# Transposing batch 1's first attention half by DMA, with later value loads and an earlier second pass, in a Sinkhorn-attention and gated-FFN kernel

## The chip, the cores and the metric

The kernel runs on one core of a Trainium2 chip. The metric is the device time of one execution in microseconds, the median of several runs; lower is better. Durations below come from one profiled execution.

## The reference

The first half is block-sorted attention over 4 batches, 8 heads, 768 positions, head size 64. The second half is a gated FFN on its output, read as 3072 tokens of 512.

```python
for _ in range(5):                      # P = sort_net, 8 x 8 for each batch and head
    P = exp(P - max(P)); P = P / rowsum(P); P = P / colsum(P)
k_sorted, v_sorted = P applied to the 8 blocks (of 96 positions) of k and v
attn = softmax(q_block @ k_sorted_block.T / 8)      # 96 x 96, block by block
x = (attn @ v_sorted_block), heads side by side     # 3072 x 512
out = (silu(x @ w_gate) * (x @ w_val)) @ w_out      # 512 -> 1536 -> 512
```

## The kernel before

**The FFN is cut into eight passes** of 384 tokens, pass n = 2b + half for batch b. In a pass, `gate` (L382) and `value` (L400) each make one of twelve 128-row groups of the hidden layer: four matmuls that read x of the pass, transposed, from the tile `xts[(b, half)]`, one matmul for each quarter (kc = 0 to 3) of the 512 features. `outp` (L414) multiplies by w_out, for the tokens of the pass before (`outp(n - 1, ...)`), so the last output comes after the last pass, in `out_halves` (L430).

**Attention is spread between the FFN's matmuls.** A unit is a pair of heads and one half of the sequence, four units make the x of one pass, eight make a batch. A unit goes through `scores` (L294, tile qk), `exps` (L314, ScalarE), `av` (L325: matmuls into av_ps, then reciprocal and product on VectorE into the tile st, L339 and L341), and then a transposition of st into one quarter of `xts`. There are two ways to transpose: `xtr` (L355) does it with four TensorE transposes (L352) and a VectorE copy; `x_dma` (L363) with one transposing DMA from SyncE's queue (L367). Batch 0 and batch 1's first half (units 0 to 3) use `xtr`; batch 1's second half and batches 2 and 3 use `x_dma`. Feature quarter kc of `xts` comes from unit kc of the half.

**Keys, queries and values.** `kq_chunk` (L239, tile tkq) mixes keys and rearranges queries of batch 1 in three pairs of chunks, each pair 64 matmuls, with one PSUM tile emptied by VectorE and one by ScalarE. `v_chunk` (L269, tile tv) mixes batch 1's values in four chunks of 16 matmuls, which read `vch`, a copy of the values with the positions innermost; GpSimd writes vch (`copy_v`, L117, run at L124). For batches 2 and 3 keys and values are loaded as pairs, `v_pair_chunk` mixes the values, and the queries go another way: `q_cast` (L370) casts them DRAM to DRAM into q_scr with GpSimd's DMA queue, in runs of 64 elements, and `q_dma` (L374) transposes q_scr into kqtq from SyncE's queue.

**Order.** TensorE's and GpSimd's instructions run in the order in which they are written. `merge` (L570) writes it: the main list is the FFN's pass, each entry with a cost (0.65 for a gate or value group, 0.87 for a third of an output tile), and a side entry is placed behind the main entry with which the summed cost reaches its due time. `units`, `kqs` and `vs` give the side entries; L609 sets the due times of pass 1, the subject here. PSUM tiles with tag "a" or "b" have one buffer each, so a matmul into one waits until the last content has been read. The order on VectorE, ScalarE and SyncE from pass 0 on is the scheduler's. GpSimd's queue, in order: copies of batch 1's values into vch (L596), the loads of the key pair (L598), of values 2 and 3 (L599), the two query casts (L601), and the four copies of the value pair into vch (L611).

Of the kernel before, what the change touches and what calls it, by code (L numbers as in the profile page):

```python
# [9 lines left out]
FP32 = mybir.dt.float32  # L10
BF16 = mybir.dt.bfloat16
# [6 lines left out]
def kernel(  # L18
# [11 lines left out]
    nc = tc.nc  # L30

    B, H, S, D = q.shape
    NB = sort_net.shape[-1]
    C = S // NB
    BH = B * H
    H2 = H // 2
    scale = 1.0 / float(D) ** 0.5
    N_ITER = 5
    DM = moe_w_gate.shape[0]
# [4 lines left out]
    R = H * NB  # L44

    k_nat = k.rearrange("b h (j c) d -> b (h j) c d", c=C)
    q_nat = q.rearrange("b h (j c) d -> b (h j) c d", c=C)
    v_nat = v.rearrange("b h (j c) d -> b (h j) c d", c=C)
# [5 lines left out]
    const = ctx.enter_context(tc.tile_pool(name="const", bufs=1))  # L54
    natp = ctx.enter_context(tc.tile_pool(name="natp", bufs=2))
    vnp = ctx.enter_context(tc.tile_pool(name="vnp", bufs=1))
    kqp = ctx.enter_context(tc.tile_pool(name="kqp", bufs=2))
    vtp = ctx.enter_context(tc.tile_pool(name="vtp", bufs=2))
    ssp = ctx.enter_context(tc.tile_pool(name="ssp", bufs=3))
    xtp = ctx.enter_context(tc.tile_pool(name="xtp", bufs=4))  # L60
    wpool = ctx.enter_context(tc.tile_pool(name="wpool", bufs=1))
    hpool = ctx.enter_context(tc.tile_pool(name="hpool", bufs=2))
# [1 line left out]
    opool = ctx.enter_context(tc.tile_pool(name="opool", bufs=3))  # L64
# [18 lines left out]
    kq_tiles = {}  # L83
    v_tiles = {}

    def kq_tile(b):
        if b not in kq_tiles:
            kq_tiles[b] = natp.tile([128, C, D], BF16, name=f"kq{b}", tag="nat")
        return kq_tiles[b]

    def load_k(b, lo, hi):
        rows = highr if b else lowr
        nc.gpsimd.dma_start(out=kq_tile(b)[rows, lo:hi, :], in_=k_nat[b, :, lo:hi, :])

    def load_k_pair():
        kq_tiles["p"] = natp.tile([128, C, D], BF16, name="kp", tag="nat")
        for u in range(2):
            nc.gpsimd.dma_start(out=kq_tiles["p"][u * R:(u + 1) * R], in_=k_nat[2 + u])

    def load_q(b, lo, hi):  # L100
        rows = lowr if b else highr
        nc.gpsimd.dma_start(out=kq_tile(b)[rows, lo:hi, :], in_=q_nat[b, :, lo:hi, :])

    def load_v(b, lo, hi):
        if b // 2 not in v_tiles:
            v_tiles[b // 2] = vnp.tile([128, C, D], BF16, name=f"v{b // 2}", tag="vn")
        u = b % 2
        nc.gpsimd.dma_start(out=v_tiles[b // 2][u * R:(u + 1) * R, lo:hi], in_=v_nat[b, :, lo:hi, :])

    def load_w(sb, dram, lo, hi):  # L110
        nc.gpsimd.dma_start(out=sb[:, :, lo:hi], in_=dram[:, :, lo:hi])
# [1 line left out]
    def load_gv(lo, hi):  # L113
        load_w(wg_sb, wg_dram, lo, hi)
        load_w(wv_sb, wv_dram, lo, hi)

    def copy_v(eng, pair, rows, s, n=4, d0=0, d1=D):  # L117
        cs = slice(s * (C // n), (s + 1) * (C // n))
        dst = vch3[rows, d0:d1, cs]
        src = v_tiles[pair][rows, cs, d0:d1]  # L120
        if eng is nc.scalar:
            eng.copy(dst, src.transpose([0, 2, 1]))  # L122
        else:
            eng.tensor_copy(dst, src.transpose([0, 2, 1]))  # L124

    ident = const.tile([128, 128], BF16)
    lowr, highr = slice(0, R), slice(R, 2 * R)
# [5 lines left out]
    HC = C // 2  # L133
    QC = C // 4
    halves = (lowr, highr)
    qk0 = natp.tile([128, C, D], BF16, name="qk0", tag="nat")
    k0 = qk0[:, 0:HC, :]
    q0 = [qk0[:, HC + t * QC:HC + (t + 1) * QC, :] for t in range(2)]
    q_runs = q.rearrange("b h (t r c) d -> b t r h (c d)", t=2, c=QC)
# [1 line left out]
    def load_q0(t):  # L141
        nc.gpsimd.dma_start(out=q0[t].rearrange("p c d -> p (c d)"), in_=q_runs[0, t])

    load_v(0, 0, HC)
    load_v(0, HC, C)
    make_identity(nc, ident)
    load_q0(0)
    for a, rows in enumerate(halves):
# [5 lines left out]
    load_q0(1)  # L154
    load_gv(512, 1024)
    load_gv(1024, DF)
    load_v(1, 0, HC)
    load_v(1, HC, C)
    for lo, hi in ((0, 64), (64, C)):
        load_k(1, lo, hi)  # L160
        load_q(1, lo, hi)
    for n in range(3):
# [28 lines left out]
    def bank_tile(name, tag="gen"):  # L191
        return psum.tile([128, 512], FP32, name=name, tag=tag, bufs=3 if tag == "gen" else 1)
# [20 lines left out]
    for lo in (0, NB // 2):  # L213
        part = slice(lo, lo + NB // 2)
# [6 lines left out]
    def drain(eng, dst, src):  # L221
        if eng == "v":
            nc.vector.tensor_copy(dst, src)  # L223
        else:
            nc.scalar.copy(dst, src)  # L225
# [3 lines left out]
    def kqt_tile(b):  # L229
        if b not in kqts:  # L230
            kqts[b] = kqp.tile([128, 2 * H2 * NB * C + 32], BF16, name=f"kqt{b}", tag="kqt")
        return kqts[b]
# [3 lines left out]
    def chunk_tile(name, n, tag):  # L236
        return pair_tile(name, tag) if n == 2 else bank_tile(name, tag)

    def kq_chunk(b, at, n, eng, tag):  # L239
        dst = kqt_tile(b)[:, 0:2 * GI * C].rearrange("p (n c) -> p n c", c=C)  # L240
        rm = rmix[b].rearrange("p a (g two) i -> p two (a g) i", two=2)
        tp = chunk_tile("tkq", n // 8, tag).rearrange("p (l n) -> p l n", n=2 * GI)
        for lc in range(n):
            for two in range(2):
                nc.tensor.matmul(tp[two * D:(two + 1) * D, lc, :],  # L245
                                 lhsT=kq_tiles[b][:, at + lc, :],
                                 rhs=rm[:, two], start=True, stop=True)
        drain(eng, dst[:, :, at:at + n], tp.transpose([0, 2, 1]))

# [41 lines left out]
    es, sts, xts = {}, {}, {}  # L291
# [32 lines left out]
    def qk(b, u, tag="b"):  # L324
        exps(b, u, *scores(b, u, tag))  # L325
# [104 lines left out]
    def out_halves(n, t3):  # L430
        b, half = divmod(n, 2)
        base = b * S + half * TW + t3 * 128
        for part, eng in ((0, "s"), (1, "v")):
            cols = slice(part * DM // 2, (part + 1) * DM // 2)
            o_ps = bank_tile("o_ps")[:, 0:DM // 2]
            for m in range(NFC):
                nc.tensor.matmul(o_ps, lhsT=h_tiles[n][:, m, ts(t3, 128)], rhs=wo_sb[m // 4][:, m % 4, cols],  # L437
                                 start=(m == 0), stop=(m == NFC - 1))
            o_sb = opool.tile([128, DM // 2], FP32, name="oh_sb", tag="oh_sb")
            drain(eng, o_sb, o_ps)  # L440
            nc.sync.dma_start(out=out[ds(base, 128), cols], in_=o_sb)

    idle_ps = bank_tile("idle_ps", "x")

# [46 lines left out]
    for b in range(1, B):  # L491
        rows = halves[b % 2]
# [46 lines left out]
    man = tc.manual_schedule(engines={ET.PE, ET.Pool})  # L539
    man.__enter__()  # L540

    def units(b, us, ats, lags=(3.1, 3.1)):
        us = list(us)
        todo = []
        for n, at in enumerate(ats):
            u, u2 = us[2 * n:2 * n + 2]
            lag = lags[n]
            held = []
            todo.append((at, lambda u=u, u2=u2, held=held: (qk(b, u, "b"), held.append(scores(b, u2, "a")))))
            todo.append((at + 1.3, lambda u2=u2, held=held: exps(b, u2, *held[0])))  # L550
            for w, tag, t in ((u, "b", 1.9), (u2, "a", 3.6)):
                if b == 0 or b == 1 and u < H2:
                    todo.append((at + t, lambda w=w, tag=tag: av(b, w, tag)))
                    todo.append((at + t + lag, lambda w=w: drain("v", *xtr(b, w))))
                else:
                    todo.append((at + t, lambda w=w, tag=tag: (av(b, w, tag), x_dma(b, w))))
        return todo

    def kqs(b, ats):
        return [(at, lambda n=n: (kq_chunk(b, n * 32, 16, "v", "b"), kq_chunk(b, n * 32 + 16, 16, "s", "a")))  # L560
                for n, at in enumerate(ats)]

    def vs(f, size, ats):
        return [(at, lambda m=m: f(1, m * size, size, "sv"[m % 2], "ba"[m % 2])) for m, at in enumerate(ats)]

    def v_pairs(ats):
        return [(at, lambda m=m: (v_pair_chunk(1, m * 16, 8, "v", "b"), v_pair_chunk(1, m * 16 + 8, 8, "s", "a")))
# [2 lines left out]
    def merge(main, side):  # L570
        done, k = 0.0, 0
        side = sorted(side, key=lambda t: t[0])
        for c, f in main:
            f()
            done += c
            while k < len(side) and side[k][0] <= done:
                side[k][1]()
                k += 1
        while k < len(side):
            side[k][1]()  # L580
            k += 1

    def ffn(n):
        todo = []
        for m in range(NFC):
            if n > 0 or m > 1:
                todo.append((0.65, lambda m=m: gate(n, m)))
            if n > 0 or m > 0:
                todo.append((0.65, lambda m=m: value(n, m)))
            ends = (7, 9, 11) if n == 1 else (3, 7, 11)  # L590
            if n > 0 and m in ends:
                for part in range(3):
                    todo.append((0.87, lambda t3=ends.index(m), part=part: outp(n - 1, t3, part)))
        return todo

    for s in range(4):  # L596
        copy_v(nc.gpsimd, 0, highr, s)
    load_k_pair()  # L598
    load_v(2, 0, C)  # L599
    load_v(3, 0, C)  # L600
    q_cast(2)  # L601
    q_cast(3)
    both = slice(0, 128)
    def q0_rest():
        q0_chunk(1, 0, 16, "s", "b")
        q0_chunk(1, 16, 8, "v", "a")

    merge(ffn(0), [(0.0, q0_rest)] + units(0, range(4, 8), (2.0, 6.6)))
    merge(ffn(1), kqs(1, (4.6, 5.9, 10.4)) + vs(v_chunk, 16, (7.2, 7.9, 8.5, 9.1))  # L609
          + units(1, range(4), (11.7, 16.4), (3.1, 2.4)))  # L610
    for s in range(4):  # L611
        copy_v(nc.gpsimd, 1, both, s)
    nc.vector.memset(kqt_tile("p")[:, 2 * GI * C:], 0.0)
# [42 lines left out]
```

## Time and profile before

| what | value |
|---|---|
| median of 3 runs (lowest to highest) | 248.76 us (248.68 to 249.51) |
| profiled execution, its own time | 248.79 us |
| its span in the trace | 246.7 us |
| TensorE, share of the span busy | 96% |
| pass 1 (first gate matmul to first gate matmul of pass 2) | 43.11 to 76.99 us |
| pass 2, likewise | 76.99 to 107.05 us |
| last matmul's group ends, last copy | 243.66, 243.68 to 244.1 us |
| software DMA queue (GpSimd's), moved | 14.16 MB |

The profile page gives busy time by engine, the span in 40 slices, the DMA queues, the chain of work that ended last, and groups of instructions by source line. The trace answers closer questions: instructions in order of time, waits and who ended them, stretches of time with DMA rates, and for each DMA the time from issue to landing. A row of the instruction listing reads: start, duration, engine, line, operation, tiles and shapes, count, and in brackets the idle time before it and what ended that.

### The profile page before, as it was taken

Reading aid. Unit: us, or ns where it says so; the run is one execution under the profiler, and the core shown is the slowest. Engines: PE = TensorE matmul, PEld = TensorE weight load, DVE = VectorE, ACT = ScalarE, POOL = GpSimd, SP = SyncE. Lnnn points to the kernel's source line nnn. Section 1 sums busy time; section 2 is a strip of 40 time slices with the busy share of each in tenths; the row PEclk is TensorE's granted clock in tenths of the full one; section 3 lists DMA queues with packets and bytes.
Section 4 is the critical chain, followed back from the end, with each engine's and each line's share of the span. In section 5 each row is a group of like instructions: output and inputs, shape, how many; then the busy total and the mean of one; then the engine's idle time right before and its main releaser. Section 6 shows DMA issues by size and latency. Waiting matters only on the chain.

```text
span 246.7 us, 6160 instructions
## 1 busy us (share of the span) xinstructions
PE 236.6 (96%) x2609; PEld 140.3 (57%) x2633; DVE 157.7 (64%) x332; ACT 109.8 (45%) x186; POOL 50.3 (20%) x44
## 2 busy tenths in 40 slices
PE   6799999998999999999999999999999999999995
PEld 6375666575555566655555655565555555555543
DVE  6786779888455685867557746755764585446700
ACT  3977653364444444354642642254245334222311
POOL 5992139990098000000000000000000000000000
PEclk9999999999999999999999999999999999999999
DMA  5989999999999195110121111112111211100122
GB/s 96 215 121 208 206 220 210 203 224 222 183 183 161 40 201 127 45 45 0 45 74 35 58 58 35 44 43 78 32 43 45 50 48 53 43 27 20 43 82 88
DMA packets 36682, 24.38 MB, mean 99 GB/s; under 512 B 27696, under 2 KB 32560, under 8 KB 36272
## 3 DMA queue, kind: packets, MB, share of 16 engines
q0 software_dynamic: 18480, 14.16, 37.6%
q1 hardware_dynamic: 18176, 9.84, 14.2%
q8 instruction: 20, 0.33, 0.5%
q14 instruction: 6, 0.05, 0.1%
HBM read 28.32 MB, written 7.86 MB: 147 GB/s over the span
## 4 chain that ended last, share of the span: by engine, by line
PE 84%; DVE 7%; issue 3%; ACT 2%; DMA 2%; DVEq 0%; POOLq 0%
PE g_ps L386 24%; PE v_ps L404 24%; PE o_ps L421 23%; PE tkq L245 3%; PE qk L308 3%; PE av_ps L335 3%; DMA v<-in_v_dram 2%; DVE st L341 2%; DVE vt L223 1%; DVE gs_sb L396 1%; PE o_ps L437 1%; DVE h L409 1%; PE idle_ps L447 1%; PE tv L276 1%; PE x_ps L352 1%
## 5 line engine op out<-in xcount | busy, mean ns | idle before, releaser
L396 DVE SCALAR_TENSOR_TENSOR gs_sb<-th_sb,g_ps 128x384 bf16<-128x384 bf16 x96 | 52.9, 551 | 46.6 <-ACT th_sb L394 43.5
L404 PE MATMUL v_ps<-xt,wv_sb 128*128 128x384 bf16 x380 | 77.3, 326 | 0.1
L386 PE MATMUL g_ps<-xt,wg_sb 128*128 128x384 bf16 x376 | 76.6, 325 | 0.2
L394 ACT ACTIVATE th_sb<-g_ps 128x384 bf16<-128x384 f32 x96 | 47.2, 491 | 57.7 <-PE g_ps L386 55.1
L421 PE MATMUL o_ps<-wo,h 128*128 128x512 bf16 x255 | 62.1, 379 | 1.3 <-issue 0.3
L409 DVE SCALAR_TENSOR_TENSOR h<-v_ps,gs_sb 128x384 bf16<-128x384 f32 x96 | 53.3, 556 | 7.1
L404 PEld LDWEIGHTS <-wv_sb 128*128 128x128 bf16 x380 | 35.4, 97 | 23.9 <-issue 1.0
L386 PEld LDWEIGHTS <-wg_sb 128*128 128x128 bf16 x376 | 35.0, 97 | 24.3 <-issue 0.6
L421 PEld LDWEIGHTS <-h 128*128 128x128 bf16 x276 | 25.8, 98 | 27.9
L426 ACT COPY o_sb<-o_ps 128x512 f32<-128x512 f32 x23 | 13.5, 586 | 45.2 <-PE o_ps L421 45.2
L124 POOL COPY vch<-v 64x1536 bf16<-64x1536 bf16 (+2 forms) x11 | 28.7, 2639 | 14.1 <-DMA v<-in_v_dram 14.0
L321 ACT ACTIVATE e_all<-qk 96x768 bf16<-96x768 f32 x30 | 22.5, 802 | 8.4 <-PE qk L308 8.4
L341 DVE TENSOR_TENSOR st<-av_ps,r_sb 96x512 bf16<-96x512 f32 x32 | 21.7, 680 | 0.2
L335 PEld LDWEIGHTS <-e_all 96*128 96x128 bf16 x256 | 11.9, 98 | 4.9 <-ACT e_all L321 0.9
L339 DVE RECIPROCAL r_sb<-av_ps 96x8 f32<-96x8 f32 x32 | 6.4, 199 | 12.3 <-PE av_ps L335 12.2
L335 PE MATMUL av_ps<-vt,e_all 96*128 96x65 bf16 x256 | 13.1, 193 | 0.1
L223 DVE CAST vt<-tv 96x1024 bf16<-96x1024 f32 (+1 forms) x9 | 9.8, 1098 | 2.6 <-PE tv L286 1.7
L225 ACT CAST vt<-tv 96x1024 bf16<-96x1024 f32 (+1 forms) x9 | 8.1, 914 | 5.5 <-PE tv L286 3.6
L447 PE MATMUL idle_ps<-warm_sb 128*128 128x512 bf16 x22 | 6.1, 381 | 0.4 <-issue 0.2
L223 DVE COPY oh_sb<-o_ps 128x256 f32<-128x256 f32 x1 | 0.4, 425 | 9.3 <-PE o_ps L437 9.3
L371 POOL DMA_DIRECT2D q_scr<-in_q_dram x2 | 5.7, 3232 | 0.0
L122 ACT COPY vch<-v 64x768 bf16<-64x768 bf16 (+1 forms) x4 | 5.5, 1387 | 0.3 <-DMA v<-in_v_dram 0.3
(80 smaller groups left out, 133.1 us busy)
## 6 DMA issues: line engine op xcount, KB each, us to landing
out_dram<-o_sb SPq DMA_DIRECT2D x23, 256.0 KB, 2.0
v<-in_v_dram POOLq DMA_DIRECT2D x4, 384.0 KB, 12.7
wg_sb<-in_moe_w_gate_dram POOLq DMA_DIRECT2D x3, 512.0 KB, 11.3
wv_sb<-in_moe_w_val_dram POOLq DMA_DIRECT2D x3, 512.0 KB, 13.1
wo<-in_moe_w_out_dram POOLq DMA_DIRECT2D x3, 512.0 KB, 15.8
kp<-in_k_dram POOLq DMA_DIRECT2D x2, 768.0 KB, 10.0
v<-in_v_dram POOLq DMA_DIRECT2D x2, 768.0 KB, 16.5
q_scr<-in_q_dram POOLq DMA_DIRECT2D x2, 768.0 KB, 25.0
```

Source lines behind the costliest of these rows:

```text
L124: eng.tensor_copy(dst, src.transpose([0, 2, 1]))
L223: nc.vector.tensor_copy(dst, src)
L321: nc.scalar.activation(e_all[:, n:n + 2, 0:4 * C], wide[0:C, :, 0:4 * C], AF.Exp, scale=scale)
L335: nc.tensor.matmul(o[:, two, i4, 0:D + 1], lhsT=e[:, i4 * C:i4 * C + 128], rhs=vt[:, 2 * g + two, half * 4 + i4, 0:D + 1], start=True, sto ...
L341: nc.vector.tensor_tensor(st.rearrange("p i two d -> p two i d"), o[0:C, :, :, 0:D], r_sb.to_broadcast([C, 2, 4, D]), op=ALU.mult)
L386: nc.tensor.matmul(g_ps, lhsT=wg_sb[:, kc, ts(m, 128)], rhs=xt[:, kc, :], start=(kc == 0), stop=(kc == NKC - 1))
L394: nc.scalar.activation(th_sb, g_ps, AF.Tanh, scale=0.5)
L396: nc.vector.scalar_tensor_tensor(gs_sb, th_sb, 1.0, g_ps, op0=ALU.add, op1=ALU.mult)
L404: nc.tensor.matmul(v_ps, lhsT=wv_sb[:, kc, ts(m, 128)], rhs=xt[:, kc, :], start=(kc == 0), stop=(kc == NKC - 1))
L409: nc.vector.scalar_tensor_tensor(h_tiles[n][:, m, :], v_ps, 0.5, gs_tiles.pop(m), op0=ALU.mult, op1=ALU.mult)
L421: nc.tensor.matmul(o_ps, lhsT=h_w[:, m, ts(t3, 128)], rhs=wo_sb[part][:, m % 4, :], start=(m == 0), stop=(m == NFC - 1))
L426: nc.scalar.copy(o_sb, o_ps)
```

## The change

Seven edits:

1. Batch 1's units 0 to 3 use `x_dma` instead of `xtr`; only batch 0 still transposes on TensorE.
2. Pass 1's due times: the three `kq_chunk` pairs move from 4.6, 5.9, 10.4 to 0.6, 3.3, 7.8; the value chunks from 7.2, 7.9, 8.5, 9.1 to 5.2, 6.5, 9.1, 10.4, with three of four emptied by ScalarE instead of two; the units from 11.7 and 16.4 to 11.0 and 15.6, with the two `av` 1.3 and 2.6 behind the scores instead of 1.9 and 3.6.
3. The loads of values 2 and 3 move behind a one-element GpSimd copy (`hold`) that reads unit 3's quarter of `xts[(1, 0)]`, so they are issued when that transposing DMA has landed. The query casts move up behind the key pair's loads.
4. Tiles for k, q and v are cut into four groups of 24 positions with 16 elements of padding between groups, so that a load's row of a partition is up to four pieces; batch 0's tiles stay dense.
5. The pool of st and r_sb has 4 buffers instead of 3.
6. In `out_halves`, the second half of the last tile is emptied as two quarters, one by VectorE with SyncE's queue, one by ScalarE with ScalarE's own DMA queue.
7. The loads' `lo, hi` are given in groups: k and q of batch 1 come as 48 + 48 positions instead of 64 + 32.

```diff
-    ssp = ctx.enter_context(tc.tile_pool(name="ssp", bufs=3))
+    ssp = ctx.enter_context(tc.tile_pool(name="ssp", bufs=4))
...
+    GC = C // 4
+    def nat_tile(pool, name, tag):
+        return pool.tile([128, 4, GC * D + 16], BF16, name=name, tag=tag)
...
+    def load_groups(tile4, rows, src, lo, hi):
+        nc.gpsimd.dma_start(out=tile4[rows, lo:hi, 0:GC * D],
+                            in_=src[:, lo * GC:hi * GC, :].rearrange("p (s c) d -> p s (c d)", c=GC))
...
-            o_sb = opool.tile([128, DM // 2], FP32, name="oh_sb", tag="oh_sb")
-            drain(eng, o_sb, o_ps)
-            nc.sync.dma_start(out=out[ds(base, 128), cols], in_=o_sb)
+            if part == 0:
+                o_sb = opool.tile([128, DM // 2], FP32, name="oh_sb", tag="oh_sb")
+                drain(eng, o_sb, o_ps)
+                nc.sync.dma_start(out=out[ds(base, 128), cols], in_=o_sb)
+                continue
+            for e, queue, lo in (("v", nc.sync, 0), ("s", nc.scalar, DM // 4)):
+                o_sb = opool.tile([128, DM // 4], FP32, name=f"oq_{e}", tag=f"oq_{e}", bufs=1)
+                drain(e, o_sb, o_ps[:, lo:lo + DM // 4])
+                queue.dma_start(out=out[ds(base, 128), ds(DM // 2 + lo, DM // 4)], in_=o_sb)
...
-    def units(b, us, ats, lags=(3.1, 3.1)):
+    def units(b, us, ats, avs=(1.9, 3.6), lag=3.1):
...
-                if b == 0 or b == 1 and u < H2:
+                if b == 0:
...
-        return [(at, lambda m=m: f(1, m * size, size, "sv"[m % 2], "ba"[m % 2])) for m, at in enumerate(ats)]
+        return [(at, lambda m=m: f(1, m * size, size, "sssv"[m], "ba"[m % 2])) for m, at in enumerate(ats)]
...
     load_k_pair()
-    load_v(2, 0, C)
-    load_v(3, 0, C)
     q_cast(2)
     q_cast(3)
...
-    merge(ffn(1), kqs(1, (4.6, 5.9, 10.4)) + vs(v_chunk, 16, (7.2, 7.9, 8.5, 9.1))
-          + units(1, range(4), (11.7, 16.4), (3.1, 2.4)))
+    merge(ffn(1), kqs(1, (0.6, 3.3, 7.8)) + vs(v_chunk, 16, (5.2, 6.5, 9.1, 10.4))
+          + units(1, range(4), (11.0, 15.6), (1.3, 2.6)))
+    hold = const.tile([1, 1], BF16)
+    nc.gpsimd.tensor_copy(hold, xts[(1, 0)][0:1, H2 - 1, 0:1])
+    load_v(2, 0, 4)
+    load_v(3, 0, 4)
     for s in range(4):
         copy_v(nc.gpsimd, 1, both, s)
```

More of the change, by code (lines that the diff above doesn't have):

```diff
@@ L84, with grouped, dense, kq_at @@
     v_tiles = {}
+    GC = C // 4
+    def nat_tile(pool, name, tag):
+        return pool.tile([128, 4, GC * D + 16], BF16, name=name, tag=tag)
+    def grouped(t):
+        return t[:, :, 0:GC * D].rearrange("p s (c d) -> p s c d", d=D)
+    def dense(t):
+        return t.rearrange("p s n -> p (s n)")[:, 0:C * D].rearrange("p (c d) -> p c d", d=D)
+    def load_groups(tile4, rows, src, lo, hi):
+        nc.gpsimd.dma_start(out=tile4[rows, lo:hi, 0:GC * D],
+                            in_=src[:, lo * GC:hi * GC, :].rearrange("p (s c) d -> p s (c d)", c=GC))
     def kq_tile(b):
         if b not in kq_tiles:
-            kq_tiles[b] = natp.tile([128, C, D], BF16, name=f"kq{b}", tag="nat")
+            kq_tiles[b] = nat_tile(natp, f"kq{b}", "nat")
         return kq_tiles[b]
+    def kq_at(b, c):
+        return grouped(kq_tiles[b])[:, c // GC, c % GC, :]
     def load_k(b, lo, hi):
-        rows = highr if b else lowr
-        nc.gpsimd.dma_start(out=kq_tile(b)[rows, lo:hi, :], in_=k_nat[b, :, lo:hi, :])
+        load_groups(kq_tile(b), highr, k_nat[b], lo, hi)
     def load_k_pair():
-        kq_tiles["p"] = natp.tile([128, C, D], BF16, name="kp", tag="nat")
         for u in range(2):
-            nc.gpsimd.dma_start(out=kq_tiles["p"][u * R:(u + 1) * R], in_=k_nat[2 + u])
+            load_groups(kq_tile("p"), slice(u * R, (u + 1) * R), k_nat[2 + u], 0, 4)
     def load_q(b, lo, hi):
-        rows = lowr if b else highr
-        nc.gpsimd.dma_start(out=kq_tile(b)[rows, lo:hi, :], in_=q_nat[b, :, lo:hi, :])
-    def load_v(b, lo, hi):
[L105 to L108, printed above, removed]
+        load_groups(kq_tile(b), lowr, q_nat[b], lo, hi)
+    def v_tile(pair):
+        if pair not in v_tiles:
+            v_tiles[pair] = nat_tile(vnp, f"v{pair}", "vn")
+        return v_tiles[pair]
+    def load_v(b, lo, hi):
+        rows = slice(b % 2 * R, (b % 2 + 1) * R)
+        if b == 0:
+            nc.gpsimd.dma_start(out=dense(v_tile(0))[rows, lo * GC:hi * GC], in_=v_nat[0, :, lo * GC:hi * GC, :])
+        else:
+            load_groups(v_tile(b // 2), rows, v_nat[b], lo, hi)
     def load_w(sb, dram, lo, hi):
@@ L119, in copy_v @@
         dst = vch3[rows, d0:d1, cs]
-        src = v_tiles[pair][rows, cs, d0:d1]
+        src = (dense(v_tiles[0])[rows, cs, d0:d1] if rows == lowr else
+               grouped(v_tiles[pair])[rows, s, :, d0:d1])
         if eng is nc.scalar:
@@ L135 @@
     halves = (lowr, highr)
-    qk0 = natp.tile([128, C, D], BF16, name="qk0", tag="nat")
+    qk0 = dense(nat_tile(natp, "qk0", "nat"))
     k0 = qk0[:, 0:HC, :]
@@ L142, in load_q0 @@
         nc.gpsimd.dma_start(out=q0[t].rearrange("p c d -> p (c d)"), in_=q_runs[0, t])
-    load_v(0, 0, HC)
-    load_v(0, HC, C)
+    load_v(0, 0, 2)
+    load_v(0, 2, 4)
     make_identity(nc, ident)
@@ L156 @@
     load_gv(1024, DF)
-    load_v(1, 0, HC)
-    load_v(1, HC, C)
-    for lo, hi in ((0, 64), (64, C)):
+    load_v(1, 0, 2)
+    load_v(1, 2, 4)
+    for lo, hi in ((0, 2), (2, 4)):
         load_k(1, lo, hi)
@@ L245, in kq_chunk @@
                 nc.tensor.matmul(tp[two * D:(two + 1) * D, lc, :],
-                                 lhsT=kq_tiles[b][:, at + lc, :],
+                                 lhsT=kq_at(b, at + lc),
                                  rhs=rm[:, two], start=True, stop=True)
@@ L546, in units @@
             u, u2 = us[2 * n:2 * n + 2]
-            lag = lags[n]
             held = []
@@ L550, in units @@
             todo.append((at + 1.3, lambda u2=u2, held=held: exps(b, u2, *held[0])))
-            for w, tag, t in ((u, "b", 1.9), (u2, "a", 3.6)):
-                if b == 0 or b == 1 and u < H2:
+            for w, tag, t in ((u, "b", avs[0]), (u2, "a", avs[1])):
+                if b == 0:
                     todo.append((at + t, lambda w=w, tag=tag: av(b, w, tag)))
```

## Prediction, made before the changed kernel was run

> **What bounds the kernel now.** First the page: busy time by engine, clock and DMA slices, then the chain's shares.
>
> ```profile
> PE 236.6 (96%) x2609; PEld 140.3 (57%) x2633; DVE 157.7 (64%) x332; ACT 109.8 (45%) x186; POOL 50.3 (20%) x44
> ...
> PEclk9999999999999999999999999999999999999999
> DMA  5989999999999195110121111112111211100122
> ...
> PE 84%; DVE 7%; issue 3%; ACT 2%; DMA 2%; DVEq 0%; POOLq 0%
> ```
>
> TensorE is busy 96% of the span, at full clock, and is 84% of the chain; its order is fixed. A microsecond less in its stream is a microsecond less at the end. The DMA engines are full for 13 of 40 slices, to about 80 us, so whatever is added to them before that queues.
>
> Second, TensorE's instructions in order of time through pass 1 (43.11 to 76.99 us, 33.88). Starts tell more than durations, as matmuls overlap: start to start, a gate or value group takes 0.65, a third of an output tile 0.87, a key chunk pair 1.13, a value chunk 0.46, a pair of scores 0.45, an av 0.25, a unit's four transposes 0.17. Pass 1 has 24, 9, 3, 4, 2, 4 and 4 of them: 15.6 + 7.8 + 3.4 + 1.85 + 0.9 + 1.0 + 0.7 = 31.25. So 2.6 us of the 33.88 are gaps. The largest are in these rows:
>
> ```profile
> 56.02 0.63 PE L276 MATMUL tv<-rmix,vch 128*128 128x64 bf16 x16
> 56.84 0.63 PE L276 MATMUL tv<-rmix,vch 128*128 128x64 bf16 x16 [0.20 <-DVE vt L223]
> ...
> 58.70 0.95 PE L245 MATMUL tkq<-rmix,kq 128*64 128x64 bf16 x48
> 60.17 0.44 PE L245 MATMUL tkq<-rmix,kq 128*64 128x64 bf16 x16 [0.52 <-issue]
> ...
> 67.80 0.34 PE L308 MATMUL qk<-kqt 64*128 64x96 bf16 x8
> 68.49 0.34 PE L308 MATMUL qk<-kqt 64*128 64x96 bf16 x8 [0.35 <-DVE st L341]
> ...
> 71.57 0.33 PE L352 MATMUL x_ps<-ident,st 96*128 96x96 bf16 x4
> 71.74 0.81 PE L404 MATMUL v_ps<-xt,wv_sb 128*128 128x384 bf16 x4
> ```
>
> The fourth value chunk starts 0.82 after the third (0.46 without a gap): it waits for VectorE to empty tag a. The third key pair takes 1.85 to the next output matmul at 60.55 (1.13 for the others): TensorE waited for nothing that is shown. The second scores pair takes 0.96 (0.45): its tag waits for unit 1's st.
>
> **What goes.** Transposes: 4 x 0.17 = **0.68**. The gap before the last transposes (output matmuls done at 75.84, start at 75.96): **0.12**. The value chunks no longer stand back to back: 0.82 - 0.46, **0.35**. The second scores: now av 1 is followed by three groups (1.95) and not by one output tile's third, so the scores into tag a come some 2.4 after av 1 starts; st was ready 1.9 after it (66.55 to 68.43). **0.51** goes, with 0.5 to spare. The third key pair: nothing in the edit is aimed at its 0.71; it could stay or go, ends 0 and 0.71. Two of three pairs have no gap, this one may keep it where it lands; I take **0.3**. The Trainium skill, "DMA: Bandwidth & Descriptors", section "Queues, rings and completion order", says that a DMA engine changes between queue rows only at packet boundaries. If that gap is TensorE's instruction fetch behind long value rows, cut rows end it, and the sum would be 0.4 better. No row here names the fetch as the cause.
>
> **What comes.** The fourth value chunk (tag a, VectorE) now has only one output third and half a scores pair before the next user of tag a: 0.46 + 0.87 + 0.1 + 0.22 = 1.65 from its start. In the trace VectorE was through with such a chunk 1.89 after its start (54.90 to 56.79) and 2.20 (56.84 to 59.04). The wait is 0.25 to 0.55, 1.1 if another 0.55 product goes first; I take **0.4**. Moving key pairs up by four units of cost: their loads were issued from 21.5 to 29.0 us and landed within 18.6, by 44.9; the first pair is now due at 44.0 and needs the first piece (41.3 or so), the second at 48.5. Values: GpSimd's copies end at 48.0, the first value chunk comes at about 51. Covers of 2.7, 3.5 and 3, so nothing, and later microsecond for microsecond if the loads slip by more. Emptying three chunks on ScalarE costs 1.01 each on an engine that is 45% busy.
>
> **The new wait.** Pass 2's first gate needs unit 3's quarter with its fourth matmul. By the sum so far pass 1 takes 33.88 - 1.56 = 32.3, so pass 2 starts at 75.4 and that matmul is at 75.9. Behind the last av stand 0.25 + 4 x 0.65 + 3 x 0.87 = 5.45, so this av starts at 70.0. In pass 2, av to the DMA's issue on SyncE took 1.8 to 2.4 us (79.50 to 81.40, 86.38 to 88.81): issue at 71.8 to 72.4. SyncE's queue also has an output tile's DMA before it (0.33) and unit 2's transpose (1.2), both earlier. Landing took 2.4 on a quiet queue, 3.8 and 4.0 (issued at 83.5 and 93.6) beside a query transpose: 74.2 to 76.4. Against 75.9 that is a cover of 1.7 to a wait of 0.5; I take a wait of **0.2**.
>
> Beside the query casts no transposing DMA stands in the trace. The nearest rows are the output DMAs issued in those casts, at 64.8 and 71.5:
>
> ```profile
> L428 SPq DMA_DIRECT2D out_dram<-o_sb x1: 368/368/368, 64.8 to 64.8; - x1
> DMA to landing us min/median/max: 5.9/5.9/5.9
> ...
> L428 SPq DMA_DIRECT2D out_dram<-o_sb x1: 332/332/332, 71.5 to 71.5; - x1
> DMA to landing us min/median/max: 6.0/6.0/6.0
> ...
> GB/s 156 158 159 159 173 178 254 316 272 374 270 278 236 174 183 149 160 160 156 158 159 159 156 153 158 153 159 159 159 151 159 157 158 160 156 159 158 267 150 146
> ```
>
> 5.9 and 6.0 instead of 2.0: **4.0 us late**. The last row is the rate from 68 to 74 us in 40 steps: 157 GB/s of casts alone, up to 374 while the output moves. So the output waited, then moved beside the casts without slowing them. Hence it counts when the casts end. The values of batches 2 and 3 moved from 58.3 to 65.8 (7.5 us at 213 GB/s) and the casts from 65.8 to 78.6 (12.8). With the values behind them the casts run from 58.3 to 71.1, to 72.3 with some of the transposes' own time (a 768 KB query transpose lands in 5.3, an eighth of it is 0.66). Units 0 and 1 (issued near 64 and 66) land late but before 73; unit 2 before 75; unit 3 is issued as the casts end. So its wait lies between 0 and 2.6 (72.1 + 2.4 + 4.0 = 78.5 against 75.9), and the value nearest is the quiet one.
>
> **Hidden.** After unit 3 lands, near 75, GpSimd issues the values: 1.1 to issue, 7.5 to move, 2 to land, 85 to 86; four copies of 2.83 end at 97. The first value pair chunk stood at 105.61 and now stands near 104. The cover is 7; the query transposes that share the DMA from 83 on (5.3 and 7.2) take less. Only copies and loads queue behind the held GpSimd instruction. Units 4 to 7 transpose beside the values, but pass 3 needs them at 105. The row pieces and padding: weights with 2 KB rows moved at the 200 to 224 GB/s of the longer rows, so nothing. The fourth st buffer keeps unit 3 from waiting for unit 0's DMA; without it, that wait would be paid.
>
> **The tail.** The last copy is 0.42 on VectorE for 256 columns; by the rows of 256 and 512 (0.425, 0.685) 128 columns take 0.3, on ScalarE 0.27. A 128 KB output lands in 1.7, a 256 KB one in 2.0, so 64 KB in about 1.55: 0.13 + 0.15 = 0.28 less. ScalarE's own DMA queue is used nowhere before; the slowest quiet landing of an output was 2.7, which would cost 0.7. I take a gain of **0.15**, ends -0.7 and 0.28.
>
> **Sum.** 0.68 + 0.12 + 0.35 + 0.51 + 0.3 - 0.4 = 1.56 in pass 1, less 0.2 for unit 3, plus 0.15 at the tail: 1.51. The profiled execution took 248.79 (span 246.7 and 2.1 around it), 0.03 over the median, so 248.79 - 1.51 = **247.3 us**. With every term at its better end 246.3; a milder set of worse ends (key gap stays, 0.55 for the value chunk) 248.0. A measurement of this kernel can tell about 0.5%, 1.24 us, so below 247.5 counts as faster and above 250.0 as slower.
>
> **Rivals.**
>
> *Unit 3 late by what outputs are late by.* 2.6 instead of 0.2: 247.3 + 2.4 = 249.7. For it: both outputs in the casts. Against: the casts should be over. 0.10.
>
> *The gaps only move.* Moved key pairs fall on a VectorE that is busy throughout 40 to 44 us, the value chunk costs 1.1, and only the transposes' 0.68 is sure: 248.0 to 249.4. 0.15.
>
> *Slower: the transposes hold up the casts.* If a transposing DMA blocks the engines for its time instead of moving beside the casts, each costs the casts between 0.66 and its whole 2.4; at 1.5, four cost 6, the casts end at 78, unit 3 lands at 80 and TensorE stands 4.1: 248.79 - 1.71 + 4.1 = 251.2 (249.7 to 256 by the ends). It decides from a landing at 77.6 on, where the 1.71 are used up, and by over 0.5% from 78.8. For it: transposes beside a query transpose took 4.0, and the casts have tiny runs. Against: the rate row, where an output rides beside the casts. 0.15.
>
> *The change does nothing it says* (units 0 to 3 still on TensorE) can't be: the branch is gone for batch 1.
>
> The forecast's own range, 246.3 to 248.0, gets 0.57, of which 0.43 lies below 247.5; 0.03 lies below 246.3. Faster: 0.43 + 0.03 = 0.46. Same: 0.14 + 0.15 + 0.06 of the first rival = 0.35. Slower: 0.15 + 0.04 = 0.19. The range that leaves out 2 in 10 is 246.2 to 250.0.
>
> **What would show it.** TensorE transposes (L352) only for batch 0, 16 fewer; pass 1 of 32 to 32.5; scores at 67 to 68 without a wait for st; a wait of some tenths for tag a before the first scores; unit 3's DMA issued near 72 and landed near 75, the casts done by 72.5; GpSimd's value copies ending near 97, ahead of the value pair chunk. I am wrong if pass 2's first gate takes far over 0.65 from its start to the next group's, if the key chunks wait for their loads, or if the last output lands later than 1.7 after its issue.

## The result, and the profile after

The changed kernel takes 247.46 us (median of 6 runs, 247.34 to 247.65), the kernel before 248.65 (6 runs, 248.39 to 249.51). The ratio is 0.9949, interval [0.9934, 0.9965]: 1.2 us less, where 1.5 were forecast (247.3). The profiled execution took 247.53, its span 245.7. The medians below leave out three executions that lie over 1.5% above the fastest of their kernel (252.02, 251.47 and 264.17). The page of the changed kernel, the lines that answer to those of before:

```profile
PE 237.1 (97%) x2617; PEld 139.4 (57%) x2617; DVE 155.9 (63%) x327; ACT 111.2 (45%) x188; POOL 51.3 (21%) x45
...
DMA  5989999999995999510121211112111211110122
...
PE 86%; DVE 6%; issue 2%; DMA 2%; ACT 2%; DVEq 0%; POOLq 0%
```

TensorE is still the bound. The DMA engines were full to slice 13 before; now they drop to half in that slice (the values are held) and are full in the three behind it. TensorE in pass 1, the rows that tell the most:

```profile
54.63 1.20 PE L269 MATMUL tkq<-rmix,kq 128*64 128x64 bf16 x64
...
59.02 0.63 PE L300 MATMUL tv<-rmix,vch 128*128 128x64 bf16 x16
59.49 1.03 PE L445 MATMUL o_ps<-wo,h 128*128 128x512 bf16 x4
60.45 0.34 PE L332 MATMUL qk<-kqt 64*128 64x96 bf16 x8
61.75 0.35 PE L332 MATMUL qk<-kqt 64*128 64x96 bf16 x8 [0.96 <-DVE vt L247]
62.03 1.90 PE L445 MATMUL o_ps<-wo,h 128*128 128x512 bf16 x8
...
66.95 0.52 PE L332 MATMUL qk<-kqt 64*128 64x96 bf16 x16
...
73.13 2.75 PE L445 MATMUL o_ps<-wo,h 128*128 128x512 bf16 x12
75.72 0.81 PE L410 MATMUL g_ps<-xt,wg_sb 128*128 128x384 bf16 x4
```

Pass 1 runs from 43.07 to 75.72, 32.65 instead of 33.88. The transposes are gone, the third key pair is in one piece, the later scores (66.95) wait for nothing, and three output thirds follow without a gap. One wait is new: the first scores take 1.58 to the next output matmul (60.45 to 62.03) where 0.45 is work. Pass 2 begins 1.27 earlier, and the last copy starts at 242.40 instead of 243.68, 1.28 earlier: what pass 1 wins arrives at the end.

The new wait of unit 3 did not show. SyncE's queue, and GpSimd's:

```profile
65.17 7.53 SPq L391 DMA_TRANSPOSE xt<-st  x3
72.74 0.58 SPq L452 DMA_DIRECT2D out_dram<-o_sb  x1
73.37 1.22 SPq L391 DMA_TRANSPOSE xt<-st  x1
```

```profile
75.74 0.18 POOL L639 COPY hold<-xt 1x1 bf16<-1x1 bf16 x1 [20.82 <-DMA xt<-st]
76.30 1.23 POOL L100 DMA_DIRECT2D v<-in_v_dram  x2 [0.38 <-POOL hold L639]
88.86 11.27 POOL L148 COPY vch<-v 128x1536 bf16<-128x1536 bf16 x4 [11.33 <-DMA v<-in_v_dram]
```

Units 0 and 1 were issued at 65.2 and 66.6 and landed 6.3 and 5.3 later, unit 2 at 70.5 and 3.3 later, unit 3 at 73.4 and 2.3 later: 75.7, against a need at 76.2. The casts' packets ended by 71. The value copies end at 100.1, the first value pair chunk starts at 104.33.

### The profile page after: what moved, and what is told of

Its sections match the earlier page's. It is cut to its first block, busy times and chain, and to the rows that moved or that the text cites. A ratio compares the mean times of both kernels' runs of the same rounds, so it can differ in the third digit from the quotient of the medians.

```text
span 245.7 us, 6163 instructions
## 1 busy us (share of the span) xinstructions
PE 237.1 (97%) x2617; PEld 139.4 (57%) x2617; DVE 155.9 (63%) x327; ACT 111.2 (45%) x188; POOL 51.3 (21%) x45
## 3 DMA queue, kind: packets, MB, share of 16 engines
q0 software_dynamic: 19632, 14.16, 38.7%
## 4 chain that ended last, share of the span: by engine, by line
PE 86%; DVE 6%; issue 2%; DMA 2%; ACT 2%; DVEq 0%; POOLq 0%
PE v_ps L428 24%; PE g_ps L410 24%; PE o_ps L445 24%; PE tkq L269 3%; PE av_ps L359 3%; PE qk L332 3%; DMA v<-in_v_dram 2%; DVE st L365 1%; DVE vt L247 1%; DVE gs_sb L420 1%; PE o_ps L461 1%; PE idle_ps L477 1%; DVE h L433 1%; PE tq L279 1%; PE tv L300 1%
## 5 line engine op out<-in xcount | busy, mean ns | idle before, releaser
L445 PE MATMUL o_ps<-wo,h 128*128 128x512 bf16 x276 | 64.4, 379 | 0.0
L148 POOL COPY vch<-v 64x1536 bf16<-64x1536 bf16 (+2 forms) x11 | 28.8, 2658 | 13.3 <-DMA v<-in_v_dram 13.3
L249 ACT CAST vt<-tv 96x1024 bf16<-96x1024 f32 (+1 forms) x10 | 9.1, 923 | 5.6 <-PE tv L310 3.6
L247 DVE CAST vt<-tv 96x1024 bf16<-96x1024 f32 (+1 forms) x8 | 8.6, 1082 | 2.2 <-PE tv L310 1.7
L477 PE MATMUL idle_ps<-warm_sb 128*128 128x512 bf16 x25 | 6.9, 382 | 0.0
```

Source lines behind the costliest of these rows:

```text
L445: nc.tensor.matmul(o_ps, lhsT=h_w[:, m, ts(t3, 128)], rhs=wo_sb[part][:, m % 4, :], start=(m == 0), stop=(m == NFC - 1))
```

## The experiments

The kernel before is itself uneven: on one chip its runs went from 247.96 to 250.06 (22 runs), on another from 247.91 to 249.33 (17). So times of kernels are compared with each other, and with the changed kernel's 247.46 and 247.47, more than with that median.

**The tail undone.**

```diff
-            for e, queue, lo in (("v", nc.sync, 0), ("s", nc.scalar, DM // 4)):
-                ...
+            drain(eng, o_sb, o_ps)
+            nc.sync.dma_start(out=out[ds(base, 128), cols], in_=o_sb)
```

> The changed kernel with the last half tile emptied as before: one VectorE copy of 256 columns and one DMA from SyncE's queue. Theory: the split tail costs time, because ScalarE's quarter copy started only when VectorE's had ended (242.72 behind 242.40 + 0.29), and the span ends 3.3 us after the last copy's start instead of 3.0. Then this kernel is 0.1 to 0.3 faster than the changed one's 247.46: 247.2 to 247.35. Rival (the tail gains 0.15, as was predicted): 247.6. Rival (nothing in it matters): 247.45.

247.35 (6 runs, 247.29 to 247.45): 0.1 below the changed kernel, at the edge of what two chips' medians can tell. The changed kernel's last copies show why nothing was won:

```profile
242.40 0.29 DVE L247 COPY oq_v<-o_ps 128x128 f32<-128x128 f32 x1 [9.33 <-PE o_ps L461]
242.72 0.33 SPq L471 DMA_DIRECT2D out_dram<-oq_v  x1
242.72 0.27 ACT L249 COPY oq_s<-o_ps 128x128 f32<-128x128 f32 x1 [1.27 <-DVE oq_v L247]
243.02 0.38 ACTq L471 DMA_DIRECT2D out_dram<-oq_s  x1
```

ScalarE's quarter copy begins only when VectorE's has ended, so the last DMA is issued 0.62 after the start of VectorE's copy, with the old tail 0.45 (242.29 to 242.74), and lands in 1.6 instead of 1.7. From the start of VectorE's last copy to the end of the execution's time it is 5.13 with the split tail and 5.11 with the old one (247.53 - 242.40, 247.40 - 242.29), as in the kernel before (248.79 - 243.68 = 5.11).

**Units 0 to 3 on TensorE again.**

```diff
-                if b == 0:
+                if b == 0 or b == 1 and u < H2:
```

> The changed kernel, but units 0 to 3 of batch 1 are transposed by TensorE and copied by VectorE again, 3.1 of cost behind their av; all due times and the order of the loads stay as changed. Theory: each unit's four transposes take 0.17 of TensorE's order, so pass 1 grows by 0.68, and by 0.1 to 0.3 of gaps before the transposes: 248.1 to 248.4. Rival (the transposes lay in gaps anyway): 247.5.

248.31 (11 runs, 248.18 to 248.68), 0.85 above the changed kernel, inside the theory's range. Its sum is right only in the transposes: in the profiled execution pass 1 takes 33.31 (46.65 to 79.96, at a clock of 1.00) against 32.65, which is 0.66 for four transposes and nothing for gaps. Where the other 0.2 of the medians lies is not shown.

**The values ahead of the casts.**

```diff
     load_k_pair()
+    load_v(2, 0, 4)
+    load_v(3, 0, 4)
     q_cast(2)
...
-    nc.gpsimd.tensor_copy(hold, xts[(1, 0)][0:1, H2 - 1, 0:1])
-    load_v(2, 0, 4)
-    load_v(3, 0, 4)
```

> The changed kernel, but the values of batches 2 and 3 are loaded ahead of the query casts, as before the change, with nothing held. Theory: the casts then end near 78.5, units 2 and 3 are issued to the DMA near 70.5 and 73.4, and a DMA issued in the casts lands some 4 us late, so unit 3 lands at 79 to 80, where the first gate of pass 2 needs it at 76.2: TensorE stands 2 to 4, 249.5 to 251.5. Rival (the transposes ride along at their quiet 2.3 to 4): 247.5. Rival (a transpose waits for the end of the casts, and holds them up besides): 252 or more.

252.40 (4 runs, 252.24 to 252.65), slower than the kernel before as well: ratio 1.0165 [1.0147, 1.0183]. Units 2 and 3, issued at 70.5 and 72.4, landed 6.7 and 7.0 later, still inside the casts: some 4.5 late, as the outputs had been. TensorE at pass 2's first gate, and then its clock (the third number from the end, behind the five engines' busy times):

```profile
75.70 0.49 PE L410 MATMUL g_ps<-xt,wg_sb 128*128 128x384 bf16 x2
77.28 0.32 PE L410 MATMUL g_ps<-xt,wg_sb 128*128 128x384 bf16 x1 [1.09 <-DMA xt<-st]
79.41 0.32 PE L410 MATMUL g_ps<-xt,wg_sb 128*128 128x384 bf16 x1 [1.80 <-DMA xt<-st]
```

```profile
80.00:81.00 1.00, 1.00 (x16) 0.60 (x9) 0.58 (x2) 1.00 (x3) 0.00 (x0) 0.98 1.34 196
81.00:84.00 3.00, 3.00 (x18) 1.66 (x17) 1.95 (x5) 1.14 (x2) 0.00 (x0) 0.50 0.08 28
84.00:85.00 1.00, 1.00 (x7) 0.54 (x6) 0.38 (x1) 0.17 (x1) 0.00 (x0) 0.81 0.01 1
```

2.9 us of waiting, and then the granted clock is 0.50 for three microseconds: 3 x 0.5 + 0.19 + 0.02 = 1.7 lost again. Together 4.6 of the 4.9. My theory had the wait and not the clock.

**The fourth value chunk one group earlier.**

```diff
-vs(v_chunk, 16, (5.2, 6.5, 9.1, 10.4))
+vs(v_chunk, 16, (5.2, 6.5, 9.1, 9.7))
```

> The changed kernel with the fourth value chunk due at 9.7 instead of 10.4, which puts it one value group earlier, so that VectorE has 0.65 more to empty tag a before the second unit's scores. Theory: the wait of 1.1 us before those scores (60.45 to 62.03 where 0.45 is work) falls to 0.4 or less, pass 1 takes 31.6 to 32.0, the kernel 246.4 to 246.8; if unit 3's transposing DMA then lands later than it is needed, up to 0.5 of that is lost. Rival (the wait is not VectorE's but TensorE's own fetch): 247.4.

246.36 (6 runs, 246.20 to 246.68), 1.1 below the changed kernel. The wait is gone whole:

```profile
58.61 0.63 PE L300 MATMUL tv<-rmix,vch 128*128 128x64 bf16 x16
59.07 0.81 PE L428 MATMUL v_ps<-xt,wv_sb 128*128 128x384 bf16 x4
59.72 1.03 PE L445 MATMUL o_ps<-wo,h 128*128 128x512 bf16 x3
60.68 0.51 PE L332 MATMUL qk<-kqt 64*128 64x96 bf16 x16
61.13 1.90 PE L445 MATMUL o_ps<-wo,h 128*128 128x512 bf16 x8
```

**The changed kernel again, beside three others.**

> The changed kernel itself once more, beside the next three on one chip, as their yardstick. Expected: the ratio to the kernel before that it had, 0.9949 within 0.001; that is about 1.2 us less than the kernel before.

247.47 (6 runs, 247.35 to 247.81): its time is the same to 0.01, but the ratio is 0.9969 [0.9957, 0.9980], outside what I expected, since the kernel before had a median of 248.44 here.

**The early chunk and the old tail together** (both edits above).

> The changed kernel with the fourth value chunk due at 9.7 and with the last half tile emptied as before, by one VectorE copy and one DMA. Theory: the two gains add: 1.0 from the value chunk and 0.1 from the tail, 1.1 below the changed kernel on the same chip. Rival (the tail as changed is the better one): 0.8 to 0.9 below. Rival (the gain of the early chunk is lost to unit 3's DMA): 0.5 below.

246.37 (5 runs), 1.1 below the changed kernel, but equal to the early chunk alone. So the tail is worth nothing either way that these runs can tell. This is the best kernel of the study: 0.9922 [0.9909, 0.9936]. In it unit 3's quarter landed just as it was needed (the held copy at 75.23, the fourth matmul at 75.2): a further gain in pass 1 would meet that DMA.

**The due times alone, on the kernel before** (L609's times as changed, the value chunks as changed, `xtr` kept with a lag of 3.1).

> The kernel before with the changed due times of pass 1 alone (and ScalarE emptying three of four value chunks); units 0 to 3 are still transposed by TensorE, 3.1 of cost behind their av, and the loads are as before. Theory: of the terms in pass 1 these stay: 0.35 and 0.51 of waits that go, 0.71 of the third key pair's gap, less 1.13 of the new wait for tag a: 0.44 faster than the kernel before, 0.3 to 0.6 with other gaps before the transposes. Rival (the key pair's gap belongs to the loads, not to the place): 0.3 slower. Rival (the whole gain comes of the due times): 1.2 faster.

248.18 (11 runs, 248.08 to 248.41), 0.26 below the median of before (ratio 0.9984 [0.9969, 1.0], which the 0.44 would fit too). The wait for tag a is there (0.96), the key pair is whole. Pass 1 takes 33.32 (43.05 to 76.37).

**The rows alone, on the kernel before** (padded groups of 24 positions, and with them the loads in pieces of 48 + 48).

> The kernel before with the tiles of k, q and v cut into four padded groups, loads in pieces of 24 positions, and nothing else. Theory: the third key pair's gap of 0.71 goes because the pair stands elsewhere, so here it stays, and the time is that of the kernel before within 0.2. Rival (shorter rows let TensorE's instructions in between the loads): the gap goes and the kernel is 0.5 to 0.7 faster.

248.11 (11 runs, 247.85 to 248.37). Neither theory: the median falls 0.33, and what goes is the spread, 0.5 instead of 2.1. In the profile the third key pair is whole.

**The kernel before once more.**

> The kernel before once more, one look. Theory: the 0.7 us at the third key pair (60.17, put down to issue) comes in some executions only, those of 248.7 and more; an execution of 248.0 to 248.4 has the key pair's 64 matmuls in one piece and a pass 1 of 34.1 instead of 33.9 + 0.0: about 33.2. Rival: the gap is always there, and the spread of the kernel before has another place.

248.24 (one run), and the key pair's row has no gap:

```profile
58.84 1.20 PE L245 MATMUL tkq<-rmix,kq 128*64 128x64 bf16 x64
...
61.81 0.51 PE L308 MATMUL qk<-kqt 64*128 64x96 bf16 x16
```

From batch 0's last transposes to the first scores of pass 2 it takes 34.09 (43.08 to 77.17), the execution profiled first 34.80 (42.94 to 77.74), so the 0.71 is there in some executions only. Pass 1 without it is 33.17 (43.25 to 76.42). (The 33.2 in the expectation is 33.9 less 0.7.)

**No padding in the changed kernel.**

```diff
-        return pool.tile([128, 4, GC * D + 16], BF16, name=name, tag=tag)
+        return pool.tile([128, 4, GC * D], BF16, name=name, tag=tag)
```

> The changed kernel without the 16 elements of padding between the groups, so that a load's row of a partition is one long piece again. Theory: TensorE's instructions again come late behind long rows in some executions: the spread of the runs grows from 0.5 to 1 or more, the median by 0 to 0.4. Rival (the padding does nothing): 247.5 with a spread of 0.5.

247.34 (6 runs, 247.29 to 247.62), with the loads in long rows again (18480 packets on GpSimd's DMA queue as before the change, 19632 with padding). The rival holds: in the changed kernel the padding does nothing. Why is not shown. Pieces of some 9 KB move beside the third key pair here too (30 packets with 0.27 MB, from 54.6 to 55.8), only that they are those of the key pair's loads and not of the values.

**No hold.**

```diff
-    hold = const.tile([1, 1], BF16)
-    nc.gpsimd.tensor_copy(hold, xts[(1, 0)][0:1, H2 - 1, 0:1])
```

> The changed kernel without the one-element copy: the values of batches 2 and 3 are issued right behind the query casts and not when unit 3's quarter has landed. Theory: they move from 71 to 78.5, unit 3's transposing DMA (issued at 73) goes beside them and lands 1 to 4 later than the 75.5 of the changed kernel; TensorE stands 0.5 to 3.5: 248 to 251. Rival (only the casts make a transpose late, not loads): 247.5.

260.75 (5 runs, 260.26 to 262.16; ratio 1.0496 [1.0467, 1.0524]): 13.3 above the changed kernel, almost four times the 3.5 that I had as the worst. Units 0 to 3, issued at 65.0, 66.4, 70.3 and 72.2, landed 10.7, 19.4, 17.5 and 16.1 later. TensorE at pass 2's first gate, and the two DMA queues from 74 to 86 us (packets, MB, share):

```profile
75.74 0.34 PE L410 MATMUL g_ps<-xt,wg_sb 128*128 128x384 bf16 x1
85.81 0.48 PE L410 MATMUL g_ps<-xt,wg_sb 128*128 128x384 bf16 x1 [9.73 <-DMA xt<-st]
87.90 0.91 PE L410 MATMUL g_ps<-xt,wg_sb 128*128 128x384 bf16 x2 [1.62 <-DMA xt<-st]
```

```profile
q0 software_dynamic: 603, 1.32, 95.3%
q1 hardware_dynamic: 941, 0.37, 38.6%
```

In 12 us only 941 packets of SyncE's queue came through beside 603 of the values, 1.6 to one. Each value packet carries 2.2 KB (1.32 MB in 603), one of SyncE's queue 0.4 KB on average, outputs among them. 941 packets in 12 us over 16 engines is one in 0.2 us for each engine. The Trainium skill, "DMA: Bandwidth & Descriptors", "Queues, rings and completion order", says that an engine takes turns between its queue rows packet by packet. Whether that is what happens here the counts don't show: strict turns between two queues that always have work would give one to one. Beside the casts a transpose was 3 to 5 us late (landed 5.3 to 7.7 after its issue instead of 2.3), beside loads 8 to 17. The waits are 9.73 and 1.62, and the clock, at 0.50 from 80 to 92, costs some 2.6 more after TensorE's return at 87.9.

**Three buffers of st.**

```diff
-    ssp = ctx.enter_context(tc.tile_pool(name="ssp", bufs=4))
+    ssp = ctx.enter_context(tc.tile_pool(name="ssp", bufs=3))
```

> The changed kernel with 3 buffers of st and r_sb, as before. Theory of the prediction: unit 3's product waits until unit 0's transposing DMA has landed (71.5 to 72), and that is paid. By the trace of the changed kernel st of unit 3 is due at 71.5 to 72.3 anyway and SyncE issues its DMA only at 73, so the cost is 0 to 0.3: 247.5 to 247.8. Rival (VectorE is held and TensorE behind it): 248 or more.

248.24 (11 runs, 247.47 to 249.06), 0.8 above the changed kernel; the rival holds in the median, though the two fastest runs (247.47 and 247.70) lose next to nothing. VectorE stands at unit 3's product until unit 0's DMA has landed, its gate product comes late, and TensorE behind it; pass 1 takes 33.45 (42.91 to 76.36), 0.80 more:

```profile
71.91 0.69 DVE L365 TENSOR_TENSOR st<-av_ps,r_sb 96x512 bf16<-96x512 f32 x1 [1.17 <-DMA xt<-st]
72.52 0.54 DVE L420 SCALAR_TENSOR_TENSOR gs_sb<-th_sb,g_ps 128x384 bf16<-128x384 bf16 x1
```

```profile
73.11 0.81 PE L428 MATMUL v_ps<-xt,wv_sb 128*128 128x384 bf16 x4 [0.66 <-DVE gs_sb L420]
```

## Why the prediction was right, and where its terms were not

The mechanism was right, and the total near it in part by luck: the third key pair gave 0.41 more than I took, the wait for tag a cost 0.73 more, and the 0.2 for unit 3 and the 0.15 for the tail came to nothing. Together that is 0.27 less than the 1.51.

| step | forecast | measured in pass 1 and at the end |
|---|---|---|
| four units' transposes off TensorE | 0.68 | 0.68; in pass 1 of the second experiment 0.66 |
| gap before the last transposes | 0.12 | gone |
| value chunks apart | 0.35 | gone |
| later scores' wait for st | 0.51 | gone (0.45 from 66.95) |
| third key pair | 0.3 | 0.71 between the two profiled executions, 0 against an execution without the gap |
| wait for tag a | -0.4 | -1.13 |
| unit 3's DMA | -0.2 | 0 |
| tail | +0.15 | nothing (5.13 against 5.11 from the last copy on) |

Pass 1 by the rows: 0.68 + 0.12 + 0.35 + 0.51 + 0.71 - 1.13 = 1.24, and it became 1.23 shorter. The two profiled executions differ by 248.79 - 247.53 = 1.26. Against an execution of before without the gap (248.24) the same sum without the 0.71 is 0.53, and pass 1 is 0.52 shorter (33.17 to 32.65). These two executions are 0.71 apart; 0.18 of that lies ahead of pass 1, whose start (43.25 and 43.07) also differs between two executions of the changed kernel (43.07 and 43.27). So part of the measured 1.2 is that the kernel before loses 0.7 us in some of its executions and the changed one did not in any of its 12.

What is left is the transposes. The due times win 0.12 + 0.35 + 0.51 and lose 1.13, and with them alone pass 1 is 33.32, 0.15 longer than without the gap; taking the transposes out then brings 0.67 (33.32 to 32.65). That is the main term of the rival "The gaps only move" (the value chunk costs 1.1, only the transposes' 0.68 is sure), which I gave 0.15. Its time, 248.0 or more, was counted from an execution with the gap, and so lay too high.

**The step that failed is the wait for tag a** ("What comes"). I took 0.4 between 0.25 and 0.55, and had named 1.1 "if another 0.55 product goes first". That is what happened, as VectorE's rows of the changed kernel show:

```profile
59.35 0.55 DVE L420 SCALAR_TENSOR_TENSOR gs_sb<-th_sb,g_ps 128x384 bf16<-128x384 bf16 x1 [0.83 <-ACT th_sb L418]
60.01 0.56 DVE L433 SCALAR_TENSOR_TENSOR h<-v_ps,gs_sb 128x384 bf16<-128x384 f32 x1
60.49 1.21 DVE L247 CAST vt<-tv 96x1024 bf16<-96x1024 f32 x1
```

The chunk stood at 59.02, but both products of the groups before it came first, and the chunk was emptied from 60.49 to 61.70. In the trace of before I had measured chunks at which VectorE owed less: emptied 0.67 and 0.99 after their start, here 1.47. I should have listed what VectorE still had to do at that moment, 0.55 + 0.56 + 1.21 from 59.35. The fourth experiment settles it: with the chunk one group (0.65) earlier, pass 1 is 1.13 shorter (31.52, from 43.29 to 74.81).

**The third key pair** was rightly kept as an open term. Its gap came in one of the two profiled executions of before, and neither due times alone nor rows alone leave a wide spread. The prediction set beside it that cut rows end the gap if long rows hold up TensorE's instruction fetch. The rows alone do narrow the spread. But without padding the changed kernel is as even, and so are the due times alone, with pieces of some 9 KB beside the third key pair in both (30 packets with 0.27 MB and 23 with 0.21 MB, from 54.6 to 55.8). What TensorE waits for in those executions, its fetch or something else, stays open.

**The new wait** came out inside its bounds, with two errors in it that nearly cancelled: unit 3 landed at 75.7, between 74.2 and 76.4. It was issued 1 us later than I had (73.4 instead of 72.4 at most), because SyncE took 2.2 for unit 2's issue instead of 1.2 and an output went between; the landing took 2.3, and the need came 0.3 later than I had. The casts' packets ended near 70.6, a little before the forecast 71.1 to 72.3.

**The rivals.** "Unit 3 late by what outputs are late by" is the third experiment's mechanism: the wait came out at 2.9, near the 2.6 of the prediction, but its price was 4.9, since the clock fell. "The transposes hold up the casts" did not happen in the changed kernel, where the casts ended early, but my ground against it was misread. The output in the rate row did slow the casts: in the 6 us from 68 to 74 they moved 6461 packets, where casts alone move 4865 in 4 us (60 to 64 in the changed kernel), so some 0.7 us of them was lost. And in the third experiment the casts gave way to the transposes: 1381 packets beside 563 of SyncE's queue in the 2 us from 71 to 73, and an end at 80.9 instead of 78.6 for the kernel before. That is an estimated 0.6 for each of four transposes, just under the rival's lower end of 0.66.

Much longer delays come beside the loads, and it is the hold that keeps units 0 to 3 out of them. I had thought of that only for units 4 to 7, of which 4 and 5 landed 10.5 and 8.9 after their issue, hidden before pass 3, and had seen the hold as a place for the loads, not as what the change stands on.

**The hidden edits.** The key loads were in time. The value copies ended at 100.1 instead of 97, with 4 us of cover left instead of 7: the loads were issued at 76.3 instead of near 75, and while they moved, the transposes of units 4 and 5 and a query transpose were issued (80.1, 82.3 and 83.6); what each of these cost them is not shown. The fourth st buffer was rightly seen as needed, worth 0.8.

## What to carry to other kernels

When a transposition goes from the bound engine to a DMA, ask what else moves in the DMA queues at that moment and what it moves in: here the same DMAs landed in 2 to 3 us on drained queues, in 5 to 8 beside casts and in up to 19 beside loads, and one small held copy decided between 247 and 261. When due times move, write down for the first user of each PSUM tile all that the emptying engine still has to do before it. And profile the kernel before twice: a gap of 0.7 that only some executions have looks like a gain of the change.

## What was not expected of the hardware

The granted clock fell to 0.50 after two waits of 1.09 and 1.80 us with a matmul of 0.32 between them (third experiment), in all four runs alike (mean clock 0.992 or 0.993), so not one long wait is needed. It fell at 81.0, 1.6 us after the second wait had ended. The Trainium skill, "TensorE: Matmul & The Clock Gate", "Part 1: The HAM clock gate (the "warmup" mystery)", puts the fall to half clock after at least one idle window of about 3.4 us; the fall to half agrees, the length does not, as the stretch from 76.2 to 79.4 is 3.2 us and has a matmul in it. In the run without the hold the clock fell at 79.4, 3.3 us after TensorE had stopped at 76.1, so there the length agrees too. In both runs it came back 5 us after the last wait had ended: at 84.4 (79.4) and at 93.1 (87.9).
